# Local and global attention with a gated convolution: scores in one product per block of queries over four key pieces

## The chip, the cores and the metric

The kernel runs on one core of one Trainium2 chip. The metric is the time of an execution on the device in microseconds (us); of the kernel before there are three such times. Besides these there is one execution taken with the hardware profiler, and every duration below is from that one.

## The reference

Eight batches of eight heads. Each head has 512 local positions and 32 global ones of width 64. A local query sees the local keys at most 32 positions away and all 32 global keys; a global query sees all 544 keys. The outputs of all heads, joined to 512 columns per position, go through a layer of 1024 hidden units with a convolution over three neighbouring positions and a sigmoid gate. In short:

```python
s_g  = scale * q_g @ k_all.T                       # k_all = [k_g, k_l]
out_g = softmax(s_g) @ v_all
s_ll = where(abs(i - j) <= 32, scale * q_l @ k_l.T, -1e9)
s_lg = scale * q_l @ k_g.T
out_l = softmax([s_lg, s_ll]) @ [v_g, v_l]
h = relu(x @ w_in)                                 # x = [out_g, out_l], heads side by side
c = conv over positions, 3 taps, zero padded, per column of h
y = (h * sigmoid(c)) @ w_out
```

## The kernel before

Work on attention goes by pairs of heads: a head's 64 columns of the two heads of a pair fill 128 partitions. There are 64 heads, so 32 pairs, four to a batch. Two heads' queries and keys come in one tile `qk` (`LQ`, line 216), the values in `vf` (`LV`, line 223), the global queries of a batch in `qgf` (`LG`, line 227).

The 512 local positions are 16 blocks of 32. `SC` (step S in the plan) makes the scores of a pair into two PSUM banks, one for each head, laid out as 128 partitions by four tiles t of 128 columns: 96 columns for the block before, the block itself and the block behind, then 32 for the global keys. It does it in three layers that add up in PSUM: one bf16 product of an identity matrix and a mask over each whole bank (line 244), eight products of 128 queries with the global keys (line 251), and 32 products of 32 queries with a run of 96 local keys (line 258). A product in f32 shows as two matmul instructions in the trace, one in fp32r or bf16 as one.

On these scores run: `MA` (M, largest value per row, VectorE, line 282), `NM` (its negative, scaled), `EX` (E, the exponential with its sum, ScalarE, line 294), `NS` (inverse of the sums, lines 310 and 311), `NP` (the product with it, line 319), `TD` (transposes, VectorE, line 304), `PV` (P, the product with the values, line 345), `UA` (copies it out, line 198), `XW` (writes it to a row buffer in DRAM, line 356). Once in a batch `G` (line 274) makes the scores of the global queries from the four `qk` tiles of the batch; `GM`, `GE`, `GN`, `GS`, `GT` (transposes on TensorE, lines 416 and 417), `GC`, `GP` (line 431), `GO` and `GW` finish them.

The second part goes by nine chunks of some 484 positions. `XR` (line 363) reads the row buffer back, `XH` and `XL` split it into two fp32r parts. `Z` (PZ, line 461) makes a column block of the hidden layer in twelve matmuls, eight blocks to a chunk; each block (a unit) then passes `RE` (469), `C1` (231), `C2` twice (480), `TH` (487), `GG` (491), `GH` and `GL`. `O` (Oa and Ob, line 515) makes an output block in twice twelve matmuls, four blocks to a chunk; `OE` and `ST` write it. Eight steps `WD`, `WA`, `WC`, `WH`, `WL` at the start load and split the weights on ScalarE and VectorE.

The order on every engine's queue is fixed when the program is built: `plan` lists the steps with costs and due times (`POS`, `POS0`, `POS1`, `TIME`), `arranged` lays them out one after the other on five queues, subject to the buffers in `SLOTS` and `LIMIT` (eight PSUM banks; five `qk` tiles), and `emit` keeps that order. `ENG` and `ENG0` say which engine takes a step that more than one could (`ENG0` up to the second batch and for the first chunk).

Of the kernel before, what the change touches and what calls it, by code (L numbers as in the profile page):

```python
# [55 lines left out]
def attn_moe(ctx: ExitStack, tc: tile.TileContext, qk_d, vw_d, qg_d, w_in_d, w_out_d, cw_d, out_d):  # L56
# [35 lines left out]
    nc.gpsimd.memset(mask[3 * SG : P, 3, 2], NEG)  # L92
# [169 lines left out]

    def G(n):


        first = n - 7
        g = [groups.setdefault(2 * (n // H) + j, {}) for j in range(2)]
        for j in range(2):
            g[j]["s0"], g[j]["s1"] = bank([P, SL], "psg0"), bank([P, SG], "psg1")
        for name, keys in (("s0", slice(KEYS, KEYS + SL)), ("s1", slice(GLOB, QK))):  # L270
            for c in range(4):
                for j in range(2):
                    rows = slice(j * D, (j + 1) * D)
                    nc.tensor.matmul(  # L274
                        g[j][name][c * SG : (c + 1) * SG], lhsT=qg[n // H][rows, c, :],
                        rhs=heads[first + 2 * c]["qk"][rows, keys], start=True, stop=True,
                    )
# [266 lines left out]
    ps=8, x=6, hb=2, qk=5, vf=6, qg=2, p=4, m=4, r=3, pt=3, nt=2, pg=2, pgt=2, og=2, t=2, o=2, g=5,  # L544
# [5 lines left out]
    GC="a", GO="a", NP="v", XH="a", XL="v", NM="a", RE="a", C1="a", GH="a", GL="v", OE="a", UA="a", GS="a",  # L550
# [3 lines left out]
    GC="a", GO="a", NP="p", XH="a", XL="v", NM="a", RE="a", C1="a", GH="a", GL="v", OE="a", UA="a", GS="v",  # L554
# [4 lines left out]
    LQ=-110.24, LG=181.07, LV=751.28, S=159.5, M=260.73, E=-8.89, NS=-42.25, NM=140.75, P=399.28, UA=-128.65,  # L559
    XW=304.2, XR=228.52, NP=55.28, TD=494.07, XH=-47.9, XL=47.25, G=-377.71, GM=60.97, GE=105.24, GN=248.34,  # L560
    GS=-389.17, GT=-376.36, GC=-65.59, GP=368.74, GO=-1.08, GW=-287.65, PZ=156.09, RE=19.77, C1=-2.75, Ca=20.86,
    Cb=215, TH=-424.97, GG=-323.17, GH=-15.92, GL=-85, Oa=-74.25, Ob=40.72, OE=196.03, ST=143.39, WD=-127.19,
    WA=269.16, WC=261.09, WH=425.7, WL=232.44,
)
POS0 = dict(
    LQ=-311.18, LG=-5.95, LV=19.96, S=259.64, M=92.14, E=-108.2, NS=-275.01, NM=235.49, P=-141.93, UA=-113.69,
    XW=-439.34, XR=157.47, NP=18.22, TD=-90.94, XH=218.79, XL=-289.98, G=323.88, GM=229.09, GE=-364.25,
    GN=-343.27, GS=-126.33, GT=-161.61, GC=461.08, GP=-269.82, GO=341.85, GW=805.6, PZ=557.37, RE=-324.71,
    C1=-202.48, Ca=198.42, Cb=-205.98, TH=57.7, GG=-93.43, GH=56, GL=-303.36, Oa=-65.35, Ob=-99.04, OE=-437.59,
    ST=-107.65, WD=-9.34, WA=-58.62, WC=197.78, WH=77.56, WL=354.86,  # L570
)
POS1 = dict(
    LQ=175.9, LG=223.37, LV=215.48, S=-310.08, M=-129.62, E=237.65, NS=-504.28, NM=239.19, P=190.54, UA=-284.1,
    XW=61.28, XR=-195.64, NP=344.76, TD=-214.01, XH=-2.72, XL=170.11, G=528.61, GM=-311.89, GE=-150.58, GN=10.6,
    GS=288.94, GT=376.28, GC=-578.16, GP=-484.82, GO=-373.88, GW=105.48, PZ=172.55, RE=533.74, C1=-738.53,
    Ca=139.5, Cb=-672.48, TH=-153.75, GG=-756.55, GH=397.94, GL=502.41, Oa=310.32, Ob=-88.83, OE=-170.97,
    ST=-642.54, WD=-95.68, WA=-274.8, WC=-19.49, WH=110.87, WL=317.54,
# [3 lines left out]
    A0=75.14, R0=-135.78, A1=388.44, R1=-281.82, A2=268.4, R=-0.16, PER=85.65, T0=153.71, Z0=-39.89, O0=313.96,  # L581
    OR0=-139.84, T1=327.74, ZR=53.45, OD=-88.97, OR=125.93, END=448.85,
# [8 lines left out]
def cost(key, e):  # L591
# [71 lines left out]
def plan(B):  # L663
# [3 lines left out]
    def op(key, i, pos, later, before=(), takes=(), uses=()):  # L667
# [250 lines left out]
def laid_out(q_l, k_l, v_l, q_g, k_g, v_g, moe_w_in, moe_conv_w, moe_w_out):  # L918
# [4 lines left out]
    def blocks(g, l, before, behind):  # L923
        l = l.reshape(B, H, NB, SG, D)
        z = np.zeros_like(l[:, :, 0])
        return [z] * before + [l[:, :, i] for i in range(NB)] + [z] * behind + [g]

    keys = np.concatenate(blocks(k_g, k_l, 1, 1), axis=2)
# [3 lines left out]
    vs = blocks(v_g, v_l, 1, 1)  # L932
# [37 lines left out]
```

## Time and profile before

| | |
|---|---|
| three runs, us | 605.37, 606.48, 608.68 |
| median, us | 606.48 |
| the profiled execution, us | 610.32 |
| its span from the first to the last instruction, us | 608.5 |
| TensorE matmul busy | 581.3 us, 96% of the span |
| VectorE busy | 394.3 us, 65% |
| ScalarE busy | 373.4 us, 61% |
| GpSimd busy | 22.1 us, 4% |

The profiled execution lies 3.84 us over the median of the three runs. PE stands for TensorE's matmuls, PEld for its weight loads, DVE for VectorE, ACT for ScalarE, POOL for GpSimd, SP for the engine that issues the DMAs. Rows of a timeline run from a start to the end of the last of the instructions that are merged in it, so neighbouring rows of pipelined matmuls overlap, and the distance of starts is the time that the work takes.

### The profile page before, as it was taken

What the parts mean: (1) busy time and instruction counts of PE and PEld (TensorE: products, weight loads), DVE (VectorE), ACT (ScalarE), POOL (GpSimd) and SP (SyncE); (2) the same over time, 40 slices, a digit from 0 to 9 for tenths busy, and PEclk for the clock granted to TensorE, in tenths of its full rate; (3) what the DMA queues carried; (4) which work ended last, traced back from release to release, by engine and by line L of the source; (5) the groups of instructions that cost most, each with busy time, mean ns of one, the idle gap of its engine ahead of it and who ended that gap; (6) DMA issues with size and microseconds to landing.
All of it is one profiled execution on the core that took longest, in us unless ns stands there. A gap on an engine that the chain in (4) does not pass through costs nothing.

```text
span 608.5 us, 20081 instructions
## 1 busy us (share of the span) xinstructions
PE 581.3 (96%) x8656; PEld 476.4 (78%) x8656; DVE 394.3 (65%) x792; ACT 373.4 (61%) x1166; POOL 22.1 (4%) x42
## 2 busy tenths in 40 slices
PE   6869679999999999999999999999999999999997
PEld 4657458888887888878887888788888888888886
DVE  1596788979871797268834885289627963573560
ACT  2764577866862797358745885388627773663551
POOL 2400320000000000000000000000000000000000
PEclk9985669999999999999999999999999999999999
DMA  9375924731344422541247223621240131110101
GB/s 352 121 252 167 415 108 153 230 106 55 102 130 120 152 71 74 161 146 61 92 123 212 58 76 112 174 84 65 56 134 18 47 108 51 49 34 33 34 0 66
DMA packets 34985, 70.07 MB, mean 115 GB/s; under 512 B 9808, under 2 KB 21584, under 8 KB 33872
## 3 DMA queue, kind: packets, MB, share of 16 engines
q1 hardware_dynamic: 34896, 68.79, 34.9%
q8 instruction: 68, 1.11, 0.8%
q14 instruction: 21, 0.17, 0.1%
HBM read 50.93 MB, written 17.84 MB: 113 GB/s over the span
## 4 chain that ended last, share of the span: by engine, by line
PE 86%; DVE 1%; ACT 1%; issue 1%; ACTq 0%
PE ps_h L461 32%; PE ps_o L515 32%; PE ps_v L345 7%; PE ps_s L251 4%; PE ps_s L258 4%; PE go L431 3%; PE ps_s L244 2%; PE psg L274 1%; PE gt L416 1%; ACT pr L294 1%; PE gt L417 0%; DVE xl L201 0%; DVE pt L304 0%; DVE wt L111 0%; DVE w_in L201 0%
## 5 line engine op out<-in xcount | busy, mean ns | idle before, releaser
L515 PE MATMUL ps_o<-g,w_out 128*128 128x484 f32 (+1 forms) x864 | 200.1, 384 | 0.4 <-issue 0.4
L461 PE MATMUL ps_h<-xh,w_in 128*128 128x486 f32 (+1 forms) x576 | 191.5, 395 | 3.1 <-ACT xh L198 3.1
L515 PEld LDWEIGHTS ps_o<-g,w_out 128*128 128x128 f32 x864 | 160.3, 188 | 28.6 <-issue 0.6
L461 PEld LDWEIGHTS ps_h<-xh,w_in 128*128 128x128 f32 x576 | 110.2, 191 | 24.6 <-ACT xh L198 4.4
L480 DVE SCALAR_TENSOR_TENSOR t<-h,cw,t 128x484 f32<-128x484 f32 (+1 forms) x144 | 102.8, 715 | 29.6 <-ACT t L231 29.0
L461 PE MATMUL ps_h<-xl,w_in 128*128 128x486 f32 (+1 forms) x288 | 112.4, 390 | 4.0 <-DVE xl L201 4.0
L294 ACT ACTIVATE pr<-ps_s,negm 128x128 f32<-128x128 f32 x256 | 90.6, 375 | 4.5 <-DVE pt L304 3.1
L282 DVE TENSOR_REDUCE negm<-ps_s 128x4 f32<-128x512 f32 x64 | 42.2, 681 | 53.1 <-PE ps_s L258 53.1
L461 PEld LDWEIGHTS ps_h<-xl,w_in 128*128 128x128 f32 x288 | 55.2, 192 | 13.3 <-DVE xl L201 4.8
L491 DVE SCALAR_TENSOR_TENSOR t<-t,h 128x484 f32<-128x484 f32 (+1 forms) x72 | 47.1, 658 | 28.2 <-ACT t L487 27.6
L345 PEld LDWEIGHTS ps_v<-pt,vf 32*64 32x64 f32 x3328 | 48.8, 135 | 15.8 <-issue 9.4
L469 ACT ACTIVATE h<-ps_h 128x486 f32<-128x486 f32 (+1 forms) x72 | 41.6, 577 | 31.7 <-PE ps_h L461 31.4
L198 ACT COPY o<-ps_o 128x484 f32<-128x484 f32 (+1 forms) x36 | 20.4, 566 | 65.5 <-PE ps_o L515 63.3
L345 PE MATMUL ps_v<-pt,vf 32*64 32x96 f32 (+3 forms) x3328 | 53.3, 247 | 6.6 <-issue 3.9
L201 DVE TENSOR_TENSOR g<-t,g 128x484 fp32r<-128x484 f32 (+1 forms) x72 | 47.5, 660 | 18.3 <-ACT g L198 16.9
L201 DVE TENSOR_TENSOR xl<-xl,xh 128x486 fp32r<-128x486 f32 (+1 forms) x36 | 24.7, 686 | 49.8 <-ACT xh L198 49.7
L294 ACT ACTIVATION_READ_ACCUMULATOR pr<-ps_s,negm 128x1 f32 x256 | 54.8, 214 | 0.0
L198 ACT CAST g<-t 128x484 fp32r<-128x484 f32 (+1 forms) x72 | 43.3, 601 | 15.6 <-DVE t L491 14.1
L251 PEld LDWEIGHTS ps_s<-qk 64*128 64x128 f32 x512 | 37.6, 222 | 18.5 <-issue 15.2
L487 ACT ACTIVATE t<-t 128x484 f32<-128x484 f32 (+1 forms) x72 | 43.7, 608 | 12.8 <-DVE t L480 12.6
L231 ACT ACTIVATE t<-h,cw 128x484 f32<-128x484 f32 (+1 forms) x72 | 50.4, 701 | 1.5 <-DVE g L201 0.9
L304 DVE STREAM_TRANSPOSE pt<-pr 128x512 f32<-128x512 f32 x64 | 43.3, 692 | 0.8 <-PE ps_v L345 0.4
(64 smaller groups left out, 474.8 us busy)
## 6 DMA issues: line engine op xcount, KB each, us to landing
qk<-qk SPq DMA_DIRECT2D x32, 560.0 KB, 4.5
vf<-vw SPq DMA_DIRECT2D x32, 448.0 KB, 4.7
row<-nt SPq DMA_DIRECT2D x32, 256.0 KB, 3.6
xl<-row SPq DMA_DIRECT2D x24, 243.0 KB, 4.0
raw<-w_in SPq DMA_DIRECT2D x4, 1024.0 KB, 9.1
raw<-w_out SPq DMA_DIRECT2D x4, 1024.0 KB, 10.6
xl<-row SPq DMA_DIRECT2D x8, 244.0 KB, 3.0
out<-o SPq DMA_DIRECT2D x4, 242.0 KB, 2.0
```

What stands on the lines that cost most here:

```text
L198: nc.scalar.copy(out=out, in_=in_) if choice(key) == "a" else eng(key).tensor_copy(out=out, in_=in_)
L201: eng(key).tensor_tensor(out=out, in0=in0, in1=in1, op=ALU.subtract)
L231: nc.scalar.activation(out=out, in_=in_, func=AF.Copy, scale=by)
L251: nc.tensor.matmul(heads[n + j]["s"][:, t, 96:P], lhsT=qk[rows, t * P : (t + 1) * P], rhs=qk[rows, GLOB:QK], start=False, stop=False)
L294: nc.scalar.activation(out=st["p"][:, t, :], in_=st["s"][:, t, :], func=AF.Exp, scale=SCALE, bias=st["m"][:, t : t + 1], accum_out=two["r" ...
L304: nc.vector.transpose(out=st["pt"][:, n % 2].rearrange("p t k q -> p (t k q)"), in_=heads[n]["p"].rearrange("p t k -> p (t k)"))
L345: nc.tensor.matmul(x, lhsT=v, rhs=p, start=k == 0, stop=k == len(work[j, b]) - 1)
L461: nc.tensor.matmul(st["z"][:, 0:n], lhsT=w[:, ft, ct, :], rhs=x, start=i == 0, stop=i == 3 * NCT - 1)
L480: nc.vector.scalar_tensor_tensor(out=st["t"], in0=st["h"][:, k : k + n], scalar=cw[:, 3 * ft + k : 3 * ft + k + 1], in1=st["t"], op0=ALU.m ...
L487: nc.scalar.activation(out=t, in_=t, func=AF.Tanh)
L491: nc.vector.scalar_tensor_tensor(out=t, in0=t, scalar=1.0, in1=h, op0=ALU.add, op1=ALU.mult)
L515: nc.tensor.matmul(ps, lhsT=w[:, mt, ft, :], rhs=g, start=ft + i == 0, stop=ft == NFT - 1 and i == 2)
```

## The change

The keys in `qk` are laid out anew: 28 blocks of 32 columns, in which the 16 local blocks stand at fixed places, eight places hold copies of the global keys, and the rest are zero. For each block of queries there are then four blocks of keys (before, itself, behind, global) at equal steps, two by two, so that one product with a stepped operand of 4 times 32 columns makes all its 128 scores. `SC` is 32 such products; the identity product, the bf16 mask and the separate products with the global keys are gone. The mask becomes an f32 tile of 128 by 256 that VectorE adds to the first and third block of 32 columns of the scores in PSUM, just ahead of `MA`'s reduction.

The `qk` tile grows from 560 to 704 KB, and four are held, not five. `G` reads the local keys in two pieces (4 times 96 and 4 times 32 columns) and its loops are turned: for each of the four head pairs c all three products, where before all pairs' products of one kind came together.

Some steps go to other engines: `NP` from VectorE (POOL in the first two batches) to ScalarE; `C1` from ScalarE to POOL; in the first two batches and the first chunk also `NM` to POOL and `GO`, `OE` and `UA` from ScalarE to VectorE. All due times are new, so that the order on all queues is another one, and some costs in the plan are (those of the attention's steps on TensorE count half as much again in the first two batches).

```diff
-KEYS = SL + SG
-GLOB = KEYS + SL + SG
-QK = GLOB + SG
+AT = [7 * (i // 4) + (0, 1, 2, 5)[i % 4] for i in range(NB)]
+GLOBAL = [7 * k + x for k in range(4) for x in (3, 6)]
+QK = SL + 28 * SG
+def sight(i):
+    before, behind = (AT[i - 1] if i else -2), (AT[i + 1] if i < NB - 1 else 24)
+    u, v = AT[i] - before, behind - before
+    assert before + u + v in GLOBAL
+    return SL + before * SG, u * SG, v * SG
...
-    mask = const.tile([P, 4, 4, SG], BF16, name="mask")
+    mask = const.tile([P, 4, 2, SG], F32, name="mask")
...
-        for j in range(2):
-            nc.tensor.matmul(
-                heads[n + j]["s"].rearrange("p t k -> p (t k)"), lhsT=same, rhs=mask.rearrange("p t k c -> p (t k c)"),
-                start=True, stop=False,
-            )
-        halves = [slice(j * D, (j + 1) * D) for j in range(2)]
-        for t in range(4):
-            for j, rows in enumerate(halves):
-                nc.tensor.matmul(
-                    heads[n + j]["s"][:, t, 96:P], lhsT=qk[rows, t * P : (t + 1) * P], rhs=qk[rows, GLOB:QK], start=False, stop=False
-                )
         for t in range(4):
             for b in range(4):
                 i, at = 4 * b + t, t * P + b * SG
-                for j, rows in enumerate(halves):
+                x, u, v = sight(i)
+                for j in range(2):
+                    rows = slice(j * D, (j + 1) * D)
+                    first = qk[rows, x : x + SG]
+                    keys = bass.AP(tensor=first.tensor, offset=first.offset, ap=[first.ap[0], [v, 2], [u, 2], [1, SG]])
                     nc.tensor.matmul(
-                        heads[n + j]["s"][b * SG : (b + 1) * SG, t, 0:96], lhsT=qk[rows, at : at + SG],
-                        rhs=qk[rows, SL + i * SG : SL + i * SG + 96], start=False, stop=t == 3,
+                        heads[n + j]["s"][b * SG : (b + 1) * SG, t].rearrange("p (a b k) -> p a b k", a=2, b=2),
+                        lhsT=qk[rows, at : at + SG], rhs=keys, start=True, stop=True,
                     )
...
-        for name, keys in (("s0", slice(KEYS, KEYS + SL)), ("s1", slice(GLOB, QK))):
-            for c in range(4):
+        for c in range(4):
+            k = heads[first + 2 * c]["qk"]
+            keys = k[:, SL:].rearrange("p (a x) -> p a x", a=4)
+            parts = (
+                ("s0", slice(0, 3 * SG), keys[:, :, 0 : 3 * SG]), ("s0", slice(3 * SG, P), keys[:, :, 5 * SG : 6 * SG]),
+                ("s1", None, k[:, QK - SG : QK]),
+            )
+            for name, at, x in parts:
                 for j in range(2):
...
     def MA(n):
         st = heads[n]
         st["m"] = small.tile([P, 4], F32, name="negm", bufs=SLOTS["m"])
+        seen = st["s"].rearrange("p t (c k) -> p t c k", c=4)[:, :, 0:3:2, :]
+        nc.vector.tensor_tensor(out=seen, in0=seen, in1=mask, op=ALU.add)
         nc.vector.tensor_reduce(out=st["m"], in_=st["s"], axis=mybir.AxisListType.X, op=ALU.max)
...
-    ps=8, x=6, hb=2, qk=5, vf=6, qg=2, p=4, m=4, r=3, pt=3, nt=2, pg=2, pgt=2, og=2, t=2, o=2, g=5,
+    ps=8, x=6, hb=2, qk=4, vf=6, qg=2, p=4, m=4, r=3, pt=3, nt=2, pg=2, pgt=2, og=2, t=2, o=2, g=5,
...
-    GC="a", GO="a", NP="v", XH="a", XL="v", NM="a", RE="a", C1="a", GH="a", GL="v", OE="a", UA="a", GS="a",
+    GC="a", GO="a", NP="a", XH="a", XL="v", NM="a", RE="a", C1="p", GH="a", GL="v", OE="a", UA="a", GS="a",
...
-    GC="a", GO="a", NP="p", XH="a", XL="v", NM="a", RE="a", C1="a", GH="a", GL="v", OE="a", UA="a", GS="v",
+    GC="a", GO="v", NP="a", XH="a", XL="v", NM="p", RE="a", C1="p", GH="a", GL="v", OE="v", UA="v", GS="v",
...
```

The tables `POS`, `POS0`, `POS1` and `TIME` of due times are replaced as a whole and not shown.

## Rows read from the trace of the kernel before

**Rows 1.** The page: busy time of each engine over the span; from the 40 slices the busy tenths of PE and the granted clock in tenths.

```profile
PE 581.3 (96%) x8656; PEld 476.4 (78%) x8656; DVE 394.3 (65%) x792; ACT 373.4 (61%) x1166; POOL 22.1 (4%) x42
...
PE   6869679999999999999999999999999999999997
...
PEclk9985669999999999999999999999999999999999
```

**Rows 2.** Busy time of each engine in stretches of the span (first column the stretch, second its length, both us, then each engine's busy us with its instructions, the granted clock, the DMA share and GB/s).

```profile
0.00:81.00 81.00, 59.24 (x1286) 44.23 (x1286) 51.87 (x105) 43.41 (x177) 18.60 (x35) 0.78 0.69 255
...
260.00:324.00 64.00, 64.00 (x1059) 52.69 (x1058) 41.58 (x89) 40.88 (x138) 0.00 (x0) 1.00 0.38 114
...
512.00:608.50 96.50, 92.81 (x421) 78.78 (x419) 45.46 (x68) 46.42 (x80) 0.20 (x2) 1.00 0.12 39
```

**Rows 3.** The waits of PE from 81 us to the end, the two longest of three: who waited for whom, us in total, times, longest.

```profile
PE ps_h L461 <- DVE xl L201: 2.1, 1, 2.1
PE ps_v L345 <- issue: 1.0, 2, 0.7
```

**Rows 4.** The timeline of PE: one S in a batch of the middle and the matmul behind it (start us, us, engine, line, operation, tiles, shape, count).

```profile
333.78 0.60 PE L244 MATMUL ps_s<-mask,same 128*128 128x512 bf16 x2
334.31 1.08 PE L251 MATMUL ps_s<-qk 64*128 64x32 f32 x16
335.33 1.00 PE L258 MATMUL ps_s<-qk 64*32 64x96 f32 x64
336.25 0.48 PE L461 MATMUL ps_h<-xh,w_in 128*128 128x486 f32 x1
```

**Rows 5.** From the chain that ended last, in order of time (start us, us, what): the global-key products of two S's that follow each other, twelve matmuls of a Z, a G and a P (a G is 32 instructions, a P 104; the count is of those that the chain took in).

```profile
324.22 1.01 PE ps_s L251 x16
326.69 1.01 PE ps_s L251 x16
...
341.80 2.66 PE ps_h L461 x12
344.46 1.08 PE psg L274 x29
...
348.40 1.50 PE ps_v L345 x71
```

**Rows 6.** Groups of PE's instructions by form from 81 us to the end: the masks (two to an S), the shortest and the longest product of P, the long ones of G (16 to a G).

```profile
L244 PE MATMUL ps_s<-mask,same 128*128 128x512 bf16 x46 | 13.9, 384 | 0.0
L345 PE MATMUL ps_v<-pt,vf 32*64 32x32 f32 x672 | 25.0, 209 | 0.7 <-issue 0.7
L345 PE MATMUL ps_v<-pt,vf 32*64 32x128 f32 x448 | 13.7, 293 | 0.1
...
L274 PE MATMUL psg<-qk,qgf 64*32 64x512 f32 x112 | 7.6, 601 | 0.0
```

**Rows 7.** The timeline of PE's weight loads: the first of those of the G in rows 5.

```profile
344.39 0.18 PEld L274 LDWEIGHTS psg<-qk,qgf 64*32 64x32 f32 x16 [0.34 <-issue]
```

**Rows 8.** Groups of VectorE's, ScalarE's and GpSimd's instructions by form: mean ns of one is the second number behind the bar (the first five from 260 to 324 us, the last two over the span).

```profile
L319 DVE TENSOR_TENSOR pr<-pr,sums 128x512 f32<-128x512 f32 x8 | 5.3, 675 | 0.0
L382 DVE TENSOR_SCALAR_CACHE_REDUCE pg<-psg 128x32 f32<-128x32 f32 x2 | 0.4, 188 | 0.0
L294 ACT ACTIVATE pr<-ps_s,negm 128x128 f32<-128x128 f32 x32 | 11.2, 371 | 0.0
L231 ACT ACTIVATE t<-h,cw 128x486 f32<-128x486 f32 x8 | 5.6, 699 | 0.0
L198 ACT COPY nt<-ps_v 128x128 f32<-128x128 f32 x16 | 3.1, 277 | 0.5 <-PE ps_v L345 0.5
L319 POOL TENSOR_TENSOR pr<-pr,sums 128x512 f32<-128x512 f32 x16 | 17.4, 1091 | 64.4 <-DVE sums L311 46.0 <-DVE sums L310 9.1 <-ACT negm L231 4.4
L83 POOL MEMSET mask<- 128x512 bf16 x1 | 0.5, 530 | 0.0
```

**Rows 9.** The timeline of ScalarE and VectorE: the first and the last steps of one unit in the stretch without attention.

```profile
514.77 0.58 ACT L469 ACTIVATE h<-ps_h 128x488 f32<-128x488 f32 x1 [1.59 <-PE ps_h L461]
518.52 0.67 DVE L491 SCALAR_TENSOR_TENSOR t<-t,h 128x486 f32<-128x486 f32 x1 [0.91 <-ACT t L487]
```

**Rows 10.** The timeline of the start: PE's first S and the start of the second, two pairs of matmuls of Z, a single one between them; SP's first read of the row buffer; VectorE's last step XL of the first chunk.

```profile
5.34 1.01 PE L244 MATMUL ps_s<-mask,same 128*128 128x512 bf16 x2 [5.34 <-POOL mask L92]
...
8.13 1.53 PE L258 MATMUL ps_s<-qk 64*32 64x96 f32 x64
9.59 1.03 PE L244 MATMUL ps_s<-mask,same 128*128 128x512 bf16 x2
...
81.76 1.01 PE L461 MATMUL ps_h<-xh,w_in 128*128 128x486 f32 x2
...
82.98 1.01 PE L461 MATMUL ps_h<-xh,w_in 128*128 128x486 f32 x2
...
57.58 0.33 SPq L363 DMA_DIRECT2D xl<-row  x1
...
80.48 0.66 DVE L201 TENSOR_TENSOR xl<-xl,xh 128x486 fp32r<-128x486 f32 x1
```

**Rows 11.** Stretches as in rows 2, chosen by the granted clock (the third entry from the end).

```profile
42.00:72.00 30.00, 26.49 (x424) 20.50 (x424) 22.02 (x33) 15.31 (x51) 4.12 (x4) 0.50 0.74 260
...
260.00:267.00 7.00, 7.00 (x246) 5.58 (x245) 2.84 (x7) 3.57 (x19) 0.00 (x0) 1.00 0.53 167
```

More of the change, by code (lines that the diff above doesn't have):

```diff
@@ L74, in attn_moe @@
     make_identity(nc, ident)
-    same = const.tile([P, P], BF16, name="same")
-    nc.gpsimd.tensor_copy(out=same, in_=ident)
-    mask = const.tile([P, 4, 4, SG], BF16, name="mask")
+    mask = const.tile([P, 4, 2, SG], F32, name="mask")
     nc.gpsimd.memset(mask, 0.0)
@@ L85, in attn_moe @@
         rows = slice(b * SG, (b + 1) * SG)
-        for k, sign in ((0, 1), (2, -1)):
+        for k, sign in ((0, 1), (1, -1)):
             nc.gpsimd.affine_select(
@@ L91, in attn_moe @@
     nc.gpsimd.memset(mask[0:SG, 0, 0], NEG)
-    nc.gpsimd.memset(mask[3 * SG : P, 3, 2], NEG)
+    nc.gpsimd.memset(mask[3 * SG : P, 3, 1], NEG)
     NCOL = ROW * B
@@ L269, in G @@
             g[j]["s0"], g[j]["s1"] = bank([P, SL], "psg0"), bank([P, SG], "psg1")
-        for name, keys in (("s0", slice(KEYS, KEYS + SL)), ("s1", slice(GLOB, QK))):
-            for c in range(4):
-                for j in range(2):
[L273 to L277, printed above, removed]
+        for c in range(4):
[6 more added lines that the diff above has]
+            for name, at, x in parts:
+                for j in range(2):
+                    rows, out = slice(j * D, (j + 1) * D), g[j][name][c * SG : (c + 1) * SG]
+                    if at:
+                        out = out.rearrange("p (a x) -> p a x", a=4)[:, :, at]
+                    nc.tensor.matmul(out, lhsT=qg[n // H][rows, c, :], rhs=x[rows], start=True, stop=True)
     def MA(n):
@@ L558 @@
 POS = dict(
[L559 to L563, printed above, removed]
+    LQ=40.87, LG=215.93, LV=-243.12, S=107.44, M=-70.51, E=5.13, NS=-78.62, NM=29.46, P=56.84, UA=-17.62,
@@ L564 @@
+    XW=130.55, XR=1.62, NP=66.53, TD=36.03, XH=3.06, XL=-78.47, G=116.57, GM=-316.88, GE=52.46, GN=-126.8,
+    GS=36.17, GT=-9.45, GC=-378.84, GP=142.18, GO=60.71, GW=-40.85, PZ=150.79, RE=268.18, C1=145.08, Ca=-140.4,
+    Cb=-113.5, TH=59.26, GG=-47.92, GH=-6.62, GL=-138.03, Oa=147.2, Ob=58.82, OE=35.95, ST=218.68, WD=203.65,
+    WA=218.1, WC=-74.47, WH=335.66, WL=135.18,
 )
 POS0 = dict(
-    LQ=-311.18, LG=-5.95, LV=19.96, S=259.64, M=92.14, E=-108.2, NS=-275.01, NM=235.49, P=-141.93, UA=-113.69,
@@ L567 @@
[L567 to L570, printed above, removed]
+    LQ=-27.84, LG=-411.01, LV=36.06, S=-155.18, M=-333.78, E=-66.6, NS=111.14, NM=-450.56, P=115.25, UA=203.11,
@@ L571 @@
+    XW=49.58, XR=114.87, NP=104.11, TD=7.74, XH=-63.01, XL=-237.35, G=50.35, GM=395.61, GE=154.22, GN=-34.91,
+    GS=76.45, GT=270.97, GC=1.63, GP=187.97, GO=494.66, GW=-467.94, PZ=-194.98, RE=-426.94, C1=-56.31,
+    Ca=-303.83, Cb=41.19, TH=98.9, GG=12.61, GH=94.13, GL=-375.53, Oa=379.49, Ob=55.01, OE=29.28, ST=-343.47,
+    WD=185.44, WA=217.46, WC=-44.54, WH=-30.1, WL=166.88,
 )
 POS1 = dict(
-    LQ=175.9, LG=223.37, LV=215.48, S=-310.08, M=-129.62, E=237.65, NS=-504.28, NM=239.19, P=190.54, UA=-284.1,
@@ L574 @@
[L574 to L577, printed above, removed]
+    LQ=-63.39, LG=301.35, LV=-335.85, S=193.3, M=77.03, E=20.47, NS=-248.75, NM=-259.8, P=113.29, UA=-43.88,
@@ L578 @@
+    XW=-158.89, XR=-54.07, NP=-38.76, TD=-137.17, XH=-242.78, XL=-129.5, G=-35.21, GM=-113.52, GE=137.51,
+    GN=-160.66, GS=-99.25, GT=71.36, GC=-144.02, GP=-27.71, GO=-126.33, GW=45.2, PZ=-196.53, RE=160.59,
+    C1=-347.5, Ca=-48.32, Cb=3.66, TH=302.11, GG=61.24, GH=-381.31, GL=-125.69, Oa=6.05, Ob=-16.32, OE=-249.32,
+    ST=-157.23, WD=-338.43, WA=368.5, WC=-177.51, WH=182.59, WL=368.35,
 )
 TIME = dict(
-    A0=75.14, R0=-135.78, A1=388.44, R1=-281.82, A2=268.4, R=-0.16, PER=85.65, T0=153.71, Z0=-39.89, O0=313.96,
@@ L582 @@
-    OR0=-139.84, T1=327.74, ZR=53.45, OD=-88.97, OR=125.93, END=448.85,
+    A0=131.07, R0=-90.01, A1=-373.5, R1=272.56, A2=429.96, R=151.66, PER=64.94, T0=274.61, Z0=-174.31,
+    O0=267.42, OR0=-83.25, T1=275.17, ZR=-32.34, OD=-0.43, OR=-1.06, END=285.22,
 )
@@ L657 @@
 PE, DVE, ACT, POOL, SP = range(5)
+COLD = ("S", "P", "G", "GT", "GP")
 STRETCH = {PE: 0.005, DVE: 0.02, "shared": 0.1, ACT: 0.02, POOL: 0.1, SP: 0.0}
@@ L681, in op @@
         occ, lat = cost(key, c)
+        if e == PE and not later and key in COLD:
+            occ, lat = occ * 3 // 2, lat * 3 // 2
         more = int(occ * STRETCH["shared" if e == DVE and key in SHARED else e])
@@ L921, in laid_out @@
     c = np.ascontiguousarray
[L923 to L928, printed above, removed]
+    keys = np.zeros((B, H, 28, SG, D), k_l.dtype)
+    keys[:, :, AT] = k_l.reshape(B, H, NB, SG, D)
+    keys[:, :, GLOBAL] = k_g[:, :, None]
+    keys = keys.reshape(B, H, 28 * SG, D)
     qs = q_l.reshape(B, H, 4, 4, SG, D).transpose(0, 1, 5, 3, 2, 4).reshape(B, H, D, SL)
@@ L931, in laid_out @@
     qk = c(qk.reshape(B, H // 2, P, QK))
-    vs = blocks(v_g, v_l, 1, 1)
+    v_l = v_l.reshape(B, H, NB, SG, D)
+    vs = [np.zeros_like(v_g)] + [v_l[:, :, i] for i in range(NB)] + [np.zeros_like(v_g), v_g]
     vw = np.stack([np.stack([vs[4 * b + k] for k in range(6)] + [vs[-1]], axis=3) for b in range(4)], axis=2)
```

6 lines of the change are left out of this document (3 added, 3 removed).

## The prediction

> **What bounds the kernel now.** I read the page first: TensorE is busy for 96% of the span, VectorE for 65%, ScalarE for 61%, and of PE's 40 slices only the first few are not full [rows 1]. The table by stretches cuts this in two. Up to 81 us PE works 59.2 us and idles 21.8 at a mean clock of 0.78, and no engine is full; from there on a batch's stretch such as 260 to 324 us has PE busy for all of its 64 us, beside 41.6 on VectorE and 40.9 on ScalarE [rows 2]. The waits of PE behind 81 us are 3.1 us in two places [rows 3]. So behind 81 us the time is the sum of what stands in PE's queue, and every microsecond taken out of it counts until another engine fills up, which has some 23 of 64 us to spare. Ahead of 81 us the time is that of chains through several engines.
>
> **Part by part: S.** Behind 81 us there are 46 masks, so 23 S's; nine lie ahead [rows 6]. One S is three layers: masks from 333.78, global keys from 334.31, local keys from 335.33, the next work at 336.25 [rows 4], that is 0.53, 1.02 and 0.92 us; two S's in a row start 2.47 us apart [rows 5]. The change drops the first two layers and makes the 64 passes of the third 128 columns wide, not 96. P's passes of 32 and 128 columns differ by 293 - 209 = 84 ns [rows 6], 0.88 ns a column, and there the wide ones read their operand in steps, so I count the stepped reading as free. 32 columns more are 28 ns; 64 passes over the array's eight tiles of 64 by 32 are eight in a row, so S takes 0.92 + 0.22 = 1.14 us. Bounds: G makes 8704 columns (16 passes of 512, 16 of 32) on the same tiles in 1.08 us [rows 5], which for 8192 columns gives 1.02; a whole P, with 104 passes of 32 to 128 columns, takes 1.50 [rows 5]. I take 1.14, from the line itself. The saving is 2.47 - 1.14 = 1.33 us, between 0.97 and 1.45; 23 times that is 30.6, between 22 and 33.
>
> **G.** It has as many columns as before, in 48 passes, not 32. But its loops now go pair by pair, and one pair's products fill only two of the eight tiles. What the array does with a product whose tile is free while an earlier one waits for its own is not in the trace as such. Its nearest row: the G shows 16 weight loads within 0.18 us, both passes of all eight long products, while the first streams have hardly begun [rows 7]. Tiles therefore take work side by side, and I take 0.2 us more a G (the eight short passes that are added, at the pace of line 258, 0.92/64 each for 16). The other end is one pair after the other: each pair has the columns that now take 1.08 us for all, so 4.3 us, 3.2 more. Seven G's lie behind 81 us (112 long passes of 16 to a G) [rows 6]: 1.4 us taken, 22 at the far end. [...]
>
> **The mask on VectorE.** 64 additions of 256 columns, one input in PSUM. Nearest rows: 188 ns for 32 columns from PSUM, 675 for a product of 512 [rows 8]; half way, 0.43 us, so 3.4 a batch. NP leaves with 8 times 0.675 = 5.4. VectorE goes from 41.6 to 39.7 us in a batch. It lengthens each head's way from S to E by 0.43 us, which costs nothing as long as PE has hidden-layer work to do; at 1.00 clock it always had [rows 2, 3].
>
> **NP to ScalarE, C1 to POOL.** NP is four passes of 128 columns a head, each between 277 (a copy) and 371 ns (E) [rows 8]: 8.9 to 11.9 us a batch. C1's eight of 699 ns leave, 5.6. ScalarE goes from 40.9 to 44 to 47 us of a batch that shrinks to some 58.5, at most 81%. C1 on POOL lies between the memset of 512 columns, 0.53, and the product of 512, 1.09 [rows 8]; I take 0.8. In a unit, h is held from 514.77 to 519.19, 4.4 us [rows 9]; two are held, and Z's come 2.66 us apart at the closest [rows 5], so the chain may last 5.3. With C1 at 1.09 it lasts 4.8, still covered. If POOL and VectorE hold each other up by a whole C1, 5.9 would be over by 0.6 every second unit, only where Z's follow each other. I allow 1 us in all for such waits; the far end is 8. [...]
>
> **DMA and four tiles.** 144 KB more for each of 32 pairs, at a DMA share of 0.38 in a batch [rows 2]: hidden. With four tiles no load of the next batch starts before G has read all four; G at 344.5 comes 8 us behind the batch's last S, which ended at 336.3, and its first S's stood at 324 [rows 4, 5]; with some 64 us to a batch [rows 2] there are over 40 us from G to the next S, for a load that is under way for a few. Hidden too, save at the start.
>
> **The start.** At the low clock an S takes 9.59 - 5.34 = 4.25 us, of which the local keys 1.46 [rows 10]; after, 1.46 + 0.44 = 1.9. Nine S's give PE back 21 us. Most of it buys nothing: an S gave two heads in 4.25 us, 2.1 each, while ScalarE, which now has E and NP (4 times 371 and 4 times 277 ns), needs 2.6 a head. VectorE gets the mask for 18 heads, 7.7 us, and UA for nine pairs (four copies of 277), 10, in a stretch where it works 51.9 of 81 us [rows 2]. The bounds are therefore 21 faster and 18 slower. Between the first reading of the row buffer, at 57.6, and the last XL, at 80.5, lie 23 us for four short steps [rows 10]: the order, not the work, sets this, and a new order may shorten or lengthen it. I take a third of PE's 21 us and some of that gap, 8 us faster, as PE stood in front of work in part of the stretch only.
>
> **Sum.** Profiled execution 610.3 - 30.6 (S) - 8 (start) + 1.4 (G) + 1 (waits) = 574.1. It lies 3.8 us above the median of the runs, so 570.3.
>
> **Rivals.** First, the start comes out well: its 23 us gap shrinks, 16 us more; 554. For it: PE idles 21.8 us there; against it: VectorE gets more work. Second, G runs pair by pair, or the start loses 10 us: 570 + 20 = 590. The row of loads speaks against G, not strongly; VectorE's load speaks for a late start. Third, the change doesn't do what it says, because an operand in four pieces is read so slowly that S keeps its 2.4 us: 570 + 30 + 3 for the mask and the longer G = 603; P's rows speak against it. Fourth, slower than before: the clock. From 42 to 72 us PE was busy 26.5 of 30 us with attention's small products, and the granted clock was 0.50; the three S's from 260 to 267 left it at 1.00 [rows 11]. At the low clock three matmuls of a Z take 82.98 - 81.76 = 1.22 us [rows 10], twelve 4.9; at the high one 2.66 [rows 5]. Each microsecond at the low clock thus loses 0.46. If the new order puts a batch's S's, P's and GP together, so that the clock falls in every batch, the gain of 36 us is gone from 79 us at the low clock on, 11 a batch; 15 a batch, 105 in all, give 618. Against it: dropping the layers makes the S run shorter.
>
> **How the numbers follow.** Forecast 570 (560 to 583): 0.55. First rival, 554 (542 to 560): 0.18. Second, 590 (583 to 600): 0.17. Third, 603 (600 to 610): 0.05. Fourth, over 610: 0.05. The range has to leave out 2 in 10: 548 to 592 cuts the ends of the first and second rival and leaves out the other two. 0.5% of 606.5 is 3.0 us, about what a measurement of this kernel can tell from no change: faster by more, under 603.4, the forecast, both first rivals and a part of the third, 0.92; within it 0.03; slower 0.05.
>
> **What would show it.** Right: PE busy near 540 us, S's in a row 1.0 to 1.2 us apart, G near 1.3, PE full behind the start with waits under 6 us, ScalarE near 45 us in a batch. Wrong: an S of 1.5 us or more, a G of 3 to 4 us, PE waiting for RE's or GL's tiles where Z's follow each other, a granted clock of 0.50 behind 90 us, or a first full Z later than 81 us.

## The result and the profile after

The kernel after takes 590.43 us (median of 4 runs, 588.23 to 591.86), the kernel before 607.58 (605.37 to 609.52) beside it: a ratio of 0.972, 95% interval 0.966 to 0.977. The gain is 17 us, not the 36 forecast. The profiled run after took 589.30 us with a span of 587.5; it lies 1.1 us below its median, that of before 2.7 above its own, so the two spans differ by 21.0.

The page of the kernel after, with the lines that answer to [rows 1]:

```profile
PE 541.6 (92%) x8208; PEld 449.7 (77%) x8208; DVE 406.5 (69%) x846; ACT 391.3 (67%) x1296; POOL 65.4 (11%) x113
...
PE   4573599999997999999999999999999999999997
...
PEclk9596599999998999999999999999999999999999
```

PE works 39.7 us less, but the span shrank by 21.0: PE's time without work grew from 27.2 to 45.9 us, mostly in the first slices. A cut at the first full Z (from there on the matmuls of the hidden layer follow each other without a long wait, and PE becomes the bound) separates the two (busy time of each engine by stretch, in the columns of [rows 2]). The kernel before, cut at 81.2 us:

```profile
0.00:81.20 81.20, 59.25 (x1287) 44.24 (x1287) 52.07 (x106) 43.61 (x177) 18.60 (x35) 0.78 0.69 254
81.20:608.50 527.30, 522.08 (x7370) 432.19 (x7370) 342.27 (x687) 329.82 (x990) 3.48 (x7) 1.00 0.31 94
```

The kernel after, cut at 71.3 us, where its first full Z starts:

```profile
0.00:71.30 71.30, 36.81 (x1076) 27.34 (x1076) 54.40 (x126) 45.12 (x159) 7.45 (x37) 0.71 0.80 298
71.30:587.50 516.20, 504.77 (x7132) 422.38 (x7132) 352.06 (x721) 346.20 (x1137) 57.95 (x77) 0.99 0.34 104
```

The start is 9.9 us shorter, the rest 11.1. In the rest PE works 17.3 us less and stands idle for 11.4 us, not 5.2.

The clock in the first line of each pair, 0.78 and 0.71, needs care. The traces have no record of the granted clock ahead of 31.0 us (before) and 9.5 us (after), and a stretch without a record counts as 1.00 in these means. The work there goes at the pace of the low level (0.50 in this column): before, an S takes 4.25 us [rows 10], against 2.47 [rows 5], and two S's where the record says 0.50 start 4.28 us apart (54.41 and 58.69 us); after, the first three S's take 5.04 us, against 2.86 in a row later. By the records the clock stands at its high level (1.00) for 13.7 of the first 81.2 us before, and for 20.5 of the first 71.3 us after.

The chain that ended last of the kernel after, in the columns of [rows 5]: one S alone, a G, three S's in a row, a P.

```profile
148.19 1.09 PE ps_s L258 x64
...
270.83 3.09 PE psg L282 x42
...
303.64 2.86 PE ps_s L258 x179
...
346.81 1.50 PE ps_v L352 x72
```

S fell from 2.47 us to 1.09 alone and 2.86/3 = 0.95 in a row; P is what it was. G grew from 1.08 us [rows 5] to 3.04 to 3.09, wherever it stands behind the start.

The waits of PE in the kernel after from 71.4 us to the end, as in [rows 3]:

```profile
PE ps_v L352 <- issue: 2.8, 5, 1.0
PE ps_s L258 <- issue: 2.7, 1, 2.7
PE ps_h L468 <- DVE xl L208: 2.0, 1, 2.0
PE ps_h L468 <- ACT pr L301: 1.1, 1, 1.1
PE go L438 <- issue: 1.0, 1, 1.0
```

They are 9.6 us in many small places, and only 1.1 of it waits for ScalarE, which took over NP.

Groups by form over the whole span of the kernel after, one line each of VectorE and ScalarE: the mask addition and NP (mean ns of one is the second number behind the bar).

```profile
L288 DVE TENSOR_TENSOR ps_s<-ps_s,mask 128x256 f32<-128x256 f32 x64 | 26.9, 421 | 18.6 <-PE ps_s L258 18.4
...
L324 ACT ACTIVATE pr<-pr,sums 128x128 f32<-128x128 f32 x256 | 80.5, 407 | 2.9 <-DVE sums L317 2.0 <-DVE sums L318 0.8
```

### The profile page after: what moved, and what is told of

Same layout as the page of the kernel before. It is cut to its first block, busy times and chain, and to the rows that moved or that the text cites. A ratio compares the mean times of both kernels' runs of the same rounds, so it can differ in the third digit from the quotient of the medians.

```text
span 587.5 us, 19573 instructions
## 1 busy us (share of the span) xinstructions
PE 541.6 (92%) x8208; PEld 449.7 (77%) x8208; DVE 406.5 (69%) x846; ACT 391.3 (67%) x1296; POOL 65.4 (11%) x113
## 3 DMA queue, kind: packets, MB, share of 16 engines
q8 instruction: 64, 1.05, 0.7%
## 4 chain that ended last, share of the span: by engine, by line
PE 83%; DVE 7%; issue 5%; DMA 2%; ACT 2%; SPq 1%; POOL 0%; DVEq 0%; ACTq 0%; POOLq 0%
PE ps_h L468 32%; PE ps_o L522 32%; PE ps_v L352 7%; PE psg L282 5%; PE ps_s L258 4%; PE go L438 2%; DMA qk<-qk 1%; ACT pr L301 1%; PE gt L423 1%; DMA raw<-w_out 1%; DVE t L487 1%; DVE negm L289 1%; DVE wt L118 1%; DVE xl L208 1%; DVE nt L205 1%
## 5 line engine op out<-in xcount | busy, mean ns | idle before, releaser
L522 PEld LDWEIGHTS ps_o<-g,w_out 128*128 128x128 f32 x864 | 162.3, 190 | 28.4 <-issue 1.6
L240 POOL TENSOR_SCALAR t<-h,cw 128x484 f32<-128x484 f32 (+1 forms) x72 | 57.7, 802 | 435.9 <-ACT h L476 307.1
L324 ACT ACTIVATE pr<-pr,sums 128x128 f32<-128x128 f32 x256 | 80.5, 407 | 2.9 <-DVE sums L317 2.0
L498 DVE SCALAR_TENSOR_TENSOR t<-t,h 128x484 f32<-128x484 f32 (+1 forms) x72 | 48.9, 685 | 26.3 <-ACT t L494 26.1
L468 PEld LDWEIGHTS ps_h<-xl,w_in 128*128 128x128 f32 x288 | 55.0, 191 | 12.1 <-DVE xl L208 4.0
L352 PE MATMUL ps_v<-pt,vf 32*64 32x64 f32 (+3 forms) x3328 | 53.8, 245 | 10.8 <-issue 10.3
L476 ACT ACTIVATE h<-ps_h 128x486 f32<-128x486 f32 (+1 forms) x72 | 42.0, 583 | 27.2 <-PE ps_h L468 25.5
L258 PE MATMUL ps_s<-qk 64*32 64x128 f32 x2048 | 39.5, 295 | 14.7 <-issue 9.3
L258 PEld LDWEIGHTS ps_s<-qk 64*32 64x32 f32 x2048 | 31.9, 113 | 21.5 <-issue 12.8
L289 DVE TENSOR_REDUCE negm<-ps_s 128x4 f32<-128x512 f32 x64 | 44.3, 692 | 3.3
```

What stands on the lines that cost most here:

```text
L240: nc.gpsimd.tensor_scalar(out=out, in0=in_, scalar1=by, scalar2=0.0, op0=ALU.mult, op1=ALU.add)
L258: nc.tensor.matmul(heads[n + j]["s"][b * SG : (b + 1) * SG, t].rearrange("p (a b k) -> p a b k", a=2, b=2), lhsT=qk[rows, at : at + SG], r ...
L324: nc.scalar.activation(out=p[:, t], in_=p[:, t], func=AF.Copy, scale=r[:, t : t + 1])
L352: nc.tensor.matmul(x, lhsT=v, rhs=p, start=k == 0, stop=k == len(work[j, b]) - 1)
L468: nc.tensor.matmul(st["z"][:, 0:n], lhsT=w[:, ft, ct, :], rhs=x, start=i == 0, stop=i == 3 * NCT - 1)
L498: nc.vector.scalar_tensor_tensor(out=t, in0=t, scalar=1.0, in1=h, op0=ALU.add, op1=ALU.mult)
```

## The experiments

The G of the kernel after goes pair by pair, with three products a pair (384, 128 and 32 columns). The prediction took its cost at 0.2 us; it is 2.0. My theory: one tile of the array takes only so many products, a third one to the same tile waits, and all that stands behind it in TensorE's queue waits too. Its rivals: TensorE starts matmuls strictly in program order; the products in pieces are slow in themselves; G is hidden beside other waits.

**g_by_kind.** The kernel after with G's loops turned: each kind of product over all four pairs.

```diff
-        for c in range(4):
...
-            for name, at, x in parts:
+        for c, kind in [(c, kind) for kind in range(3) for c in range(4)]:
```

> The changed kernel with G's loops by kind of product again: all four pairs' long products, then the middle ones, then the short ones, in the new layout with its pieces and stepped writes. Theory 1 (a tile takes one product in work and one behind it, and a third one blocks everything behind it in the queue): G falls from 3.09 to 1.2 to 1.4 us, seven full-clock G's give back 12 to 13 us, 590 goes to 575 to 578. Theory 2 (the pieces and the stepped writes are slow in themselves): G stays at 3 us and the time within 2 us of 590. Theory 3 (G is hidden, the loss lies in the start and the order): G falls, the time does not.

Measured: 581.04 us (576.46 to 583.43), ratio 0.954 [0.948, 0.959] to before, 9.4 us under the kernel after. G in its chain:

```profile
386.22 1.14 PE psg L284 x40
```

The same instructions in another order take 1.14 us: the pieces are not slow, and G is not hidden as a whole. But 7 times 1.95 us are 13.7, not 9.4, and 581.0 lies above the theory's 575 to 578. The profile says where a part went (the profiled execution is the slowest of the four, 2.4 us over their median); its stretch behind its first full Z (70.5 us), and the three 10 us stretches behind 80 us in which the clock was under 0.97:

```profile
70.50:581.60 511.10, 495.70 (x7132) 416.97 (x7132) 351.30 (x721) 345.36 (x1137) 58.55 (x76) 0.99 0.34 105
...
180.00:190.00 10.00, 10.00 (x160) 8.30 (x159) 8.39 (x17) 5.15 (x21) 0.00 (x0) 0.86 0.81 275
...
290.00:300.00 10.00, 8.73 (x143) 7.28 (x149) 3.36 (x6) 3.42 (x10) 0.00 (x0) 0.83 0.59 153
...
350.00:360.00 10.00, 7.75 (x195) 6.84 (x195) 3.35 (x5) 3.42 (x12) 0.00 (x0) 0.84 0.73 210
```

PE's idle time there rose from 11.4 to 15.4 us, and PE worked 9.1 us less, not 13.7. The kernel after has one such stretch (0.83 from 180 to 190 us); the 3 us behind the first full Z are at the low level in both. At 0.83 a stretch of 10 us holds 3.4 at the low level (0.50); with 0.46 lost a microsecond, the prediction's estimate from a Z at either level (4.9 us and 2.66), that is some 1.6 us of work each, 3 for the two more.

**g_short_first** (pair by pair, 32 columns first, 384 last) and **g_two_pairs** (two pairs at a time, kind by kind):

```diff
+        for c, kind in [(c, kind) for c in range(4) for kind in (2, 1, 0)]:
...
+        for c, kind in [(2 * half + i, kind) for half in range(2) for kind in range(3) for i in range(2)]:
```

> The changed kernel with G pair by pair, but in each pair the 32-column product first, then 4 times 32, then 4 times 96 columns. Theory 1: the third product to a tile is the long one and waits only for the short ones, some 0.1 to 0.25 us a pair, so the long ones of the four pairs run side by side: G 1.3 to 1.9 us, the time 576 to 582. Strict order of starts (a pair's last pass starts before the next pair's first): G stays between 2.5 and 4.3 us, 585 to 600.

> The changed kernel with G by two pairs at a time, by kind within them. Theory 1: the block of 0.68 us that the trace shows for each of four pairs comes twice, not four times: G 1.6 to 1.9 us, the time 579 to 582. Theory 2: 3 us and 590.

Measured: 582.57 us (581.45 to 583.52), 0.957 [0.952, 0.962], and 581.81 (580.16 to 584.86), 0.956 [0.951, 0.961]. A G in the chain of g_short_first, and of g_two_pairs:

```profile
383.88 2.12 PE psg L284 x31
```

```profile
387.01 1.75 PE psg L284 x44
```

The second is as the theory has it. The first lies between the theory and its rival, and outside the range of either. The three orders differ less in time (581.0, 581.8 and 582.6 us) than seven of their G's would have it (1.14, 1.75 and 2.12 us, so 4.3 and 6.9 us apart); with some 3 us to either side of a median this neither shows nor excludes that part of G is hidden.

**before_g_by_pair.** The kernel before with G's two loops turned, so that it too goes pair by pair, with two products a pair (512 and 32 columns).

```diff
-        for name, keys in (("s0", slice(KEYS, KEYS + SL)), ("s1", slice(GLOB, QK))):
-            for c in range(4):
+        for c in range(4):
+            for name, keys in (("s0", slice(KEYS, KEYS + SL)), ("s1", slice(GLOB, QK))):
```

> The kernel before with G's two loops turned, pair by pair: the 512-column product and the 32-column one of a pair, then the next pair. Theory 1: only two products to a tile, the second fits behind the first, nothing blocks: G stays at 1.1 to 1.3 us and the time at 606 to 609. Strict order of starts: a pair holds the queue for 0.9 us, G 3.4 to 3.8, seven times 2.5 us more: 622 to 627.

Measured: 607.88 us (605.5 to 614.56), 1.001 [0.997, 1.004] to before. G in its chain:

```profile
349.26 1.12 PE psg L274 x27
```

1.12 us against 1.08: going pair by pair costs nothing where a pair has two products. It is the third that does. That rules out a strict order of starts, which by the estimate in the expectation would have made this G 3.4 to 3.8 us.

What holds the queue is seen in the G at 390.1 us of the kernel after. The timeline of its weight loads, to set beside [rows 7]:

```profile
390.10 0.14 PEld L282 LDWEIGHTS psg<-qk,qgf 64*32 64x32 f32 x4 [0.34 <-ACT h L476]
...
390.77 0.47 PEld L282 LDWEIGHTS psg<-qk,qgf 64*32 64x32 f32 x12 [0.21 <-issue]
391.45 0.47 PEld L282 LDWEIGHTS psg<-qk,qgf 64*32 64x32 f32 x12 [0.21 <-issue]
392.13 0.47 PEld L282 LDWEIGHTS psg<-qk,qgf 64*32 64x32 f32 x12 [0.21 <-issue]
```

Before, 16 loads of all eight long products came within 0.18 us; now each pair's come 0.68 us after those of the pair ahead, and three such steps and one pair are the 3.09 us. PE's products under way from 390.78 to 390.86 us, by form:

```profile
L282 PE MATMUL psg<-qk,qgf 64*32 64x384 f32 x4 | 0.8, 495 | 0.0
L282 PE MATMUL psg<-qk,qgf 64*32 64x128 f32 x2 | 0.3, 269 | 0.0
```

and from 390.95 to 391.05 us:

```profile
L282 PE MATMUL psg<-qk,qgf 64*32 64x384 f32 x2 | 0.5, 507 | 0.0
L282 PE MATMUL psg<-qk,qgf 64*32 64x128 f32 x4 | 0.4, 269 | 0.0
L282 PE MATMUL psg<-qk,qgf 64*32 64x32 f32 x4 | 0.2, 191 | 0.0
```

Every product is two passes (two matmul instructions), and a pair's products go to two tiles, six passes to each. In the first view the second pass of the first pair's long products still counts (two of the four long ones), its first 128-column passes have begun, and so have the second pair's long ones, while the first pair's 32-column passes begin later, in the second view. So the next pair gets on at 390.77 us, when a pair's third passes start, while the fourth, fifth and sixth still wait: one pass in work and three behind it is the most that a tile is seen to take here. Two products, four passes, fit at once: in before_g_by_pair all four pairs' first loads come within 0.22 us.

```profile
349.19 0.22 PEld L274 LDWEIGHTS psg<-qk,qgf 64*32 64x32 f32 x16 [0.34 <-issue]
```

In g_two_pairs the second half gets on 0.68 us after the first (weight loads from 386.94 and from 387.62 us), as long as a pair's third passes took to start in the kernel after (390.10 to 390.77 us). A rival is a limit on all waiting passes together, whatever their tile. The three traces, counted this way, speak against it: in the kernel after eight waiting passes (four to each of two tiles) hold the queue, while in g_two_pairs twelve (three to each of four tiles) and in before_g_by_pair eighteen (three to each of six) let the next product on. In these three the count goes by tile.

In g_short_first 41 of the 48 loads come within 0.63 us, so the second and the third pair do get on early, as this count wants, but passes of the fourth stand 0.32 us apart (384.63 to 384.95 us):

```profile
383.81 0.63 PEld L284 LDWEIGHTS psg<-qk,qgf 64*32 64x32 f32 x41 [0.34 <-ACT h L478]
384.63 0.10 PEld L284 LDWEIGHTS psg<-qk,qgf 64*32 64x32 f32 x1 [0.19 <-issue]
384.95 0.35 PEld L284 LDWEIGHTS psg<-qk,qgf 64*32 64x32 f32 x6 [0.22 <-issue]
```

I have no reason for that, and it is left open.

The two views, with the second pair's first passes ahead of the first pair's last, and the 1.12 us of before_g_by_pair do not agree with starts strictly in program order.

**after_old_s.** The order, engines and four tiles of the kernel after, with the layout, the scores and the G of before.

```diff
-QK = SL + 28 * SG
+QK = GLOB + SG
...
+            nc.tensor.matmul(
+                heads[n + j]["s"].rearrange("p t k -> p (t k)"), lhsT=same, rhs=mask.rearrange("p t k c -> p (t k c)"),
+                start=True, stop=False,
+            )
...
-        nc.vector.tensor_tensor(out=seen, in0=seen, in1=mask, op=ALU.add)
```

> The kernel after with its order, its engines and its four tiles, but with the scores, the layout of keys and the global scores of the kernel before: three layers to an S, the mask by TensorE, qk tiles of 560 KB. Theory one (the order and the engines bring nothing of themselves; the start gained because an S became short): 590 + 24 S's behind the first full Z times 1.5 us (2.47 against 0.95 to 1.09) = 36, less 7 G's times 2.0 = 14, so 612, and with a first full Z as late as before, 81 us or later against 71.3, up to 10 more: 612 to 622. Theory two (the new order itself brings the start forward): first full Z at 71 to 76 us, and a time under 605, below the kernel before.

Measured: 613.33 us (610.75 to 616.55), 1.010 [1.004, 1.016]: above the kernel before (606.62 beside it). The time is the first theory's, the early first full Z (74.3 us) the second's. Its stretches:

```profile
0.00:74.30 74.30, 59.04 (x1204) 43.80 (x1204) 48.03 (x110) 43.69 (x155) 7.77 (x38) 1.00 0.74 270
74.30:609.00 534.70, 524.52 (x7452) 435.25 (x7452) 334.41 (x673) 347.42 (x1142) 57.24 (x77) 1.00 0.30 94
```

The new order and engines alone bring the first full Z from 81.2 to 74.3 us and give it all back behind it: 534.7 us, not 527.3, of which 5.0 are more waits (10.2 against 5.2) and 2.5 are one S more on this side (24, not 23). The 1.00 of the first stretch is no measurement: this trace has no record of the clock ahead of 70.3 us. The starts of two S's that follow each other:

```profile
60.06 1.04 PE L246 MATMUL ps_s<-mask,same 128*128 128x512 bf16 x2
...
64.34 1.04 PE L246 MATMUL ps_s<-mask,same 128*128 128x512 bf16 x2
```

They are 4.28 us apart, as in the kernel before where the record says 0.50, and so are the other S's ahead of the first full Z that follow each other. The profiled execution is also the fastest of the four, 2.6 us under their median.

Against after_old_s the kernel after has PE busy for 19.7 us less behind its first full Z: 24 S's times 1.38 to 1.52 are 33 to 36, less 14 for G.

**no_mask, c1_on_scalar, np_on_vector.** The first is the kernel after without the mask addition; the others are g_by_kind with one step put back on its engine of before, each in its place in the queue.

```diff
-        nc.vector.tensor_tensor(out=seen, in0=seen, in1=mask, op=ALU.add)
...
+MOVED = [dict(C1="a"), dict(C1="a")]
...
+MOVED = [dict(NP="p"), dict(NP="v")]
```

> The kernel after without VectorE's mask addition: it leaves the mask out, everything else stays in its place and order. Theory one (the 0.42 us a head lie beside TensorE's other work, as the prediction counted): 588 to 592, no difference from the 590.4 of the kernel after. Theory two (they stand on the path where ScalarE and VectorE feed TensorE, above all in the first 71 us, where 18 heads have 7.6 us of it, and at the single waits behind): 578 to 586, with the first full Z at 64 to 68 us, not 71.

Measured: 587.97 us (586.99 to 588.92), 0.968 [0.964, 0.972], 2.5 us under the kernel after, with intervals that overlap. Its stretches, with a first full Z at 66.0 us:

```profile
0.00:66.00 66.00, 38.12 (x1076) 30.73 (x1076) 47.45 (x108) 42.63 (x152) 6.70 (x36) 0.68 0.86 321
66.00:587.00 521.00, 509.05 (x7133) 425.55 (x7133) 334.97 (x675) 348.12 (x1145) 57.04 (x77) 0.98 0.33 103
```

The time is at the lower edge of the first theory's, the first full Z the second's. The mask does stand on the start's path, for 5.3 us; but the rest then takes 4.8 us longer for the same PE instructions, 4.3 of it PE's busy time at a lower mean clock. An earlier start was given back. In no_mask the clock rises to its high level at 72.0 us, so 6.0 us behind the first full Z are at the low one, against 3.0 in the kernel after, and later there are 3.4 and 6.8 us more of it, against 3.4. Why it fell there is not settled.

> The kernel of g_by_kind (581.0) with C1 back on ScalarE, in the same order. Theory one (C1 at 0.82 us on GpSimd is covered, and ScalarE has room): 579 to 584. Theory two (ScalarE, which feeds E to every pair of heads, is what TensorE now waits for at single places; 5.6 us a batch more on it): 586 to 600, with ScalarE near 54 us a batch and longer waits of TensorE behind 71 us. [...]

Measured: 581.87 us (577.84 to 583.22), 0.957 [0.950, 0.963]. No difference from g_by_kind: C1 is covered on either engine, the first theory.

> The kernel of g_by_kind (581.0) with NP back on VectorE, in GpSimd's place for the first batches as in the kernel before, in the same order. Theory one (NP at 4 times 0.41 us on ScalarE is hidden behind the start and costs at the start only): 576 to 580, gained ahead of the first full Z, where TensorE waits 9 us for ScalarE's tile. Theory two (hidden everywhere): 580 to 583. Theory three (VectorE, with the mask and NP, becomes late): 585 to 600, with TensorE waiting for VectorE's tiles behind 71 us.

Measured: 585.23 us (581.77 to 585.83), 0.962 [0.957, 0.967]: 4 us above g_by_kind, the third theory's side at its edge, with intervals that overlap. So NP on ScalarE costs nothing that can be measured, and may gain a little.

**kind_warm_s, kind_warm_sp, after_warm_sp.** Products that change no output, ahead of the first nine S's, and ahead of the first nine P's too; the last on the kernel after, the others on g_by_kind.

```diff
+            if n < 18:
+                heat(heads[n + j]["s"], WARM_S)
...
+        if n < 18:
+            for o in ps:
+                for _ in range(WARM_P):
+                    nc.tensor.matmul(o, lhsT=warm, rhs=warm.rearrange("p (t q) -> p t q", t=4), start=True, stop=True)
```

> The kernel of g_by_kind (581.0) with eight added products of 512 bf16 columns ahead of each of the first nine S's, into the tiles that S then overwrites; they change no output and stand only in the start, where TensorE idles 35 of 71 us at a mean granted clock of 0.68. At the price of the old masks (0.53 us for two) they are 2.1 us an S, 19 in all. Theory one (the shorter S lets the clock fall in the start, and the work at the low clock lies on the start's path): clock over 0.9 up to 71 us, first full Z at 60 to 67 us instead of 70.5, time 570 to 578. Theory two (ScalarE and VectorE set the start, whatever TensorE's clock): first full Z within 2 us of 70.5 or later by up to the 19 us of added work, time 580 to 598.

> As kind_warm_s, and with 16 added bf16 products of 128 columns ahead of each of the first nine P's (1.1 us a P at the pace of the masks, 9.6 in all). Theory one: the stretch of P's from 18 to 43 us too is at the high clock, first full Z at 58 to 66 us, 568 to 577, at or a little below kind_warm_s. Theory two: no earlier first full Z; 582 to 605.

Measured: 584.99 us (584.62 to 587.07), 0.964 [0.959, 0.969], and 589.20 (588.37 to 590.01), 0.969 [0.966, 0.973], with first full Z's at 72.8 and 75.8 us: the second theory. But the clock stands at its high level for 34.1 and 37.5 us ahead of them, against 17.1 in g_by_kind, so a start at the high level throughout was not tried. after_old_s, at the pace of the low level up to 70.3 us, has its first full Z at 74.3, no later than these: more of the high level did not come with an earlier first full Z.

> The kernel after, with G pair by pair as it is, and the added products of kind_warm_sp. It asks what G costs where both kernels have the same start: against kind_warm_sp. Theory one (G's two microseconds are paid in full by each of seven or eight G's behind each other, and the 9.4 us between after and g_by_kind were less only because the clock fell in more stretches of g_by_kind): 13 to 16 us above kind_warm_sp. Theory two (a third of G's time lies beside waits that are there anyway): 8 to 11 us above it.

Measured: 600.93 us (599.94 to 601.52), 0.989 [0.985, 0.993], 11.7 above kind_warm_sp, between the two theories. Behind the first full Z, the kernel after_warm_sp, and kind_warm_sp:

```profile
75.90:599.70 523.80, 513.55 (x7220) 429.08 (x7220) 352.82 (x721) 347.47 (x1137) 58.02 (x76) 0.99 0.32 102
```

```profile
75.80:587.50 511.70, 499.19 (x7220) 419.62 (x7220) 352.53 (x721) 346.53 (x1137) 58.00 (x77) 0.99 0.33 105
```

With starts that end within 0.1 us of each other PE works 14.4 us less with G by kind, and waits 2.3 us more: the rest is 12.1 us shorter. Some 1.7 of that are the clock's (at the prediction's 0.46 a microsecond: 11.1 us at the low level behind the first full Z in after_warm_sp, 7.5 in kind_warm_sp), so 10 to 12 of G's 13.7 us come out in the time. Most of G is paid, and 2 to 3 us of it only cover waits that would be there anyway. The 9.4 us of g_by_kind are less than that, by an amount within the scatter of two medians (each interval is some 3 us to either side).

## Why the prediction was wrong, step by step

- **The step that failed is G**: "I take 0.2 us more a G". It was 2.0, seven times: +14.1 us, not +1.4. The far end had been written down (3.2 a G, 22 in all) and the second rival had it with its 590, with a chance of 0.17. The row of loads [rows 7] was read as "tiles therefore take work side by side", which is true, and g_by_kind shows that a G in 48 passes can take 1.14 us; what it could not show is how many passes one tile takes, since a tile got four in a G there and the change made it six. That the second rival's 590 is the measured time is in part luck: G came to two thirds of its far end, the waits of 5.2 us more were not in it, and S and the start came out 3.7 us better than forecast. Neither reading weighed, free tiles or one pair after the other, was the right one.
- **S**: taken at 1.14 us, measured 0.95 to 1.09; 23 S's times 1.38 to 1.52 are 32 to 35 us where 30.6 were forecast. Reading the operand in pieces shows no price, as argued from P.
- **The start**: 8 us forecast, 9.9 measured. The size was right, the reason mostly not: 6.9 of it come from the order and engines (after_old_s), some 3 from the shorter S and what comes with it, the mask's 5.3 us against it included. Nor did the added products of the warm kernels, under which the clock is high for twice as long (34.1 and 37.5 us against 17.1), bring the first full Z forward (72.8 and 75.8 us against 70.5).
- **Mask, NP, C1**: the mask took 421 ns (0.43 taken), C1 0.80 us on the mean (0.8), NP 407 ns a pass, over its upper end of 371. ScalarE is busy 48.7 of the 64 us from 260 to 324, 76%, where 44 to 47 of 58.5 were forecast, 75 to 81%. None of it is a bound: no_mask, c1_on_scalar and np_on_vector move the time by 2.5, 0.8 and 4 us, all within overlapping intervals.
- **Waits**: 1 us more was allowed behind the start, 6.2 came (11.4 against 5.2 idle). The sign that I had set, "waits under 6 us behind the start", was missed at 9.6 by the list of waits. after_old_s has 10.2 idle with the old S: these waits belong to the new order and engines, not to the shorter S.
- **The sum with what was measured**: -9.9 (start) - 33.4 (S, the middle) + 1 (one S more behind the start) + 14.1 (G) + 6.2 (waits) = -22, against -21.0 between the spans. With G at 2.0 the forecast would have been 570 + 12.7 = 583, with the waits 588.
- **The clock** (fourth rival): S, P and GP did not pull it down in every batch; it is 0.99 behind 71.3 us, with 6.4 us at the low level while PE has work. In the start the high level lasts longer than before, 20.5 us against 13.7, although the means of 0.71 and 0.78 seem to say the opposite.

The version that beats the kernels before and after is G by kind: 581.04 us, 0.954 [0.948, 0.959]. The other two orders, g_two_pairs and g_short_first, cannot be told from it by their times.

## What to carry to other kernels

When small products are packed into an array's tiles, order them so that neighbours in the queue go to different tiles, and count the passes that one tile gets in a row: the same 48 passes took 1.14, 1.75, 2.12 or 3.09 us by order alone. A row that shows how much fits shows it for the number that it holds; if the change puts more there, the cost has to be carried as open, with the far end as a case of real weight. And a term that is taken near nought while its far end is half of the whole gain decides the forecast: it deserves the chance that the missing evidence gives it, not the one of the nicer reading.

## What the runs showed of the hardware that I had not expected

- Small products of one pair held up the next pair's, although those go to other tiles: in the kernel after the weight loads of the pairs came 0.68 us apart (390.77, 391.45, 392.13 us), each when the pair ahead started its third passes. Counted by tile that is one f32 pass in work and three behind it. This count, my reading of the traces, fits the kernel before (16 loads within 0.18 us), before_g_by_pair (0.22 us), g_two_pairs (0.68 us to the second half) and the kernel after, and not the last pair of g_short_first (0.32 us between its passes); what sets it is not shown.
- GpSimd's C1 took 0.68 us alone and 1.05 beside a VectorE product with two inputs. GpSimd's timeline in the kernel after (C1 at 271.78 us stands alone, at 281.48 beside two products of VectorE), and VectorE's:

```profile
271.78 0.68 POOL L240 TENSOR_SCALAR t<-h,cw 128x486 f32<-128x486 f32 x1 [0.95 <-ACT h L476]
281.48 1.05 POOL L240 TENSOR_SCALAR t<-h,cw 128x486 f32<-128x486 f32 x1 [9.02 <-DVE g L208]
...
280.69 1.30 DVE L208 TENSOR_TENSOR g<-t,g 128x486 fp32r<-128x486 f32 x2
```

C1 lost 0.37 us, where 0.51 were left of VectorE's pair; what holds it up is not shown. It costs no time here that can be measured, as c1_on_scalar shows (581.87 us against the 581.04 of g_by_kind).
- The mean granted clock of a stretch can be an empty record. after_old_s shows 1.00 ahead of its first full Z, yet its S's there are 4.28 us apart, as in the kernel before at a recorded 0.50, against 2.47 there at 1.00, and its records begin only at 70.3 us. Here the pace of an instruction that stands in both places told the level; the mean did not.
